# A fused attention and mixture-of-experts kernel: turns of y one iteration later, logits in four column quarters

## Chip, cores and metric

The kernel runs on one core of a Trainium2 chip. The metric is the device time of one execution in microseconds (us). TensorE (PE, with its weight loads as PEld), VectorE (DVE), ScalarE (ACT) and GpSimd (POOL) each work through their own instructions in order; SyncE (SP) issues most of the DMAs.

## What is computed

Linear attention with a gated state, then a layer of eight experts of which each token takes two, then a dense layer with h - tanh(h). Cut to what matters:

```python
f = 1 / (1 + exp(-f_logit))                      # q, k, v, f_logit: (4, 8, 768, 48)
for t in range(768):
    state = f[t][:, None] * state + outer(k[t], v[t])     # per batch and head
    y[t] = q[t] @ state
x = y as 3072 tokens of 384
logits = x @ w_gate                              # 8 experts
noisy = logits + log1p(exp(x @ w_noise)) * noise
top 2 of noisy, their softmax as weights
out = sum of weight * (relu(x @ w1[e]) @ w2[e]) over the two experts
h = out @ w_in;  result = (h - tanh(h)) @ w_out
```

## The kernel before

The stages are the attention (to about 162 us), the experts with two blocks of tokens each, and the dense layer. The change lies in the attention. Its 24 chunks j = 4c + b are 128 time steps of one batch b with all eight heads; heads are packed in pairs, four pairs a = 0..3 of 128 partitions (2 x 64, 48 of each 64 used).

The loop over j (L540) issues a software pipeline in the order of the code; no scheduler moves anything, since `manual_schedule` is on, so each engine's order is the order of these calls:

- `scores(j + 1)`: products of keys and queries into two PSUM banks pA (b3, b4), then DVE multiplies by the triangular mask (am).
- `scaled(j + 2)`: ACT makes exp of the accumulated decay and its inverse (epos, eneg); DVE scales the keys (kqT L325), POOL the queries (kqT L327).
- `post(n)`: POOL scatters rows of finished chunks to their experts' places in DRAM (L513), two in most iterations, more near the end.
- `decay(j + 3)`: ACT exp and ln, DVE scan (fc).
- `x_split(j - 1)`: ACT copies the turned y to f16 (xkeep L408), DVE the remainder (xkeep L409).
- when chunk j - 1 ends a group of four: `group_logits`, the product of the gate weights with y of the whole group, into bank b7, which ACT copies (lgT).
- `outputs(j)`: state times queries (L367) and am times values (L371, the two heads of a pair in the two column halves of the array) into bank b5; ACT copies to yT (L376).
- `group_rows`: the logits are turned to rows of tokens on PE and copied by ACT (lgs); `route` is a generator that picks the two experts and the places, and `advance(n)` issues a few of its steps at several places of an iteration. Its first DVE step is nl (L452), behind two ACT steps (ex).
- `key_rows(j + 1)`, `states(j)`: turned keys, their products with the values (pK, bank b6), DVE sum (tsum), POOL scaling of the state (L395). They don't exist for the last four chunks.
- `x_rows(j)`: PE turns y of chunk j into the single bank b0 (pX). It needs the copy yT of chunk j and the split of chunk j - 1, which empties b0.

Behind the loop come the split of the last chunk and the first expert products; `load_x(0, 0)`, issued by SP in iteration 21, brings the first block of expert 0 from DRAM when the scatters so far have landed, `load_x(0, 1)` the second when all have. An fp32 product is two passes of the array, so it shows as two records.

Of the kernel before, what the change touches and what calls it, by code (L numbers as in the profile page):

```python
# [8 lines left out]
F32 = mybir.dt.float32  # L9
# [5 lines left out]
AF = mybir.ActivationFunctionType  # L15
# [5 lines left out]
B, H, S, D = 4, 8, 768, 48  # L21
N, DM, NE, FF, F2 = 3072, 384, 8, 1024, 2048
NCH = S // 128
NT = B * NCH
CAP = 832
GN = 4 * 16 + NT * NE
# [45 lines left out]
def fast(ctx, tc, flag, f_cols, kq_cols, v_rows, gates, blank, w12, w_in, w_out, out):  # L72
# [179 lines left out]
    with ExitStack() as actx:  # L252
# [35 lines left out]
        wgn = gn[:, 0:64].rearrange("p (a c) -> p a c", a=4)  # L288
        nz = gn[:, 64:].rearrange("p (c b e) -> p c b e", c=NCH, b=B)
# [124 lines left out]
        def logits(g):  # L414
            y = T["yT", g]
            p = ps.tile([128, 96], F32, name="pt", tag="b7")
            for a in range(4):
                nc.tensor.matmul(p, y[:, a, 0, :], gn[:, 16 * a:16 * a + 96], start=(a == 0), stop=(a == 3))
            nc.scalar.activation(lgs[:, groups[g][0], :], p[:, :16], AF.Copy)

        def group_logits(g):
            G = len(groups[g])
            p = ps.tile([16, 4, 128], F32, name="pt", tag="b7")
            for a in range(4):
                nc.tensor.matmul(p[:, :G], wgn[:, a, :], T["yT", g][:, a, :G, :], start=(a == 0), stop=(a == 3))  # L425
            t = T["lgT", g] = work.tile([16, 4, 128], F32, name="lgT", bufs=1)
            nc.scalar.activation(t[:, :G], p[:, :G], AF.Copy)

        def group_rows(g):
            G = len(groups[g])  # L430
            j0 = groups[g][0]
            t = T.pop(("lgT", g))
            p = ps.tile([128, 4, 16], F32, name="pt", tag="b7")
            for i in range(G):
                nc.tensor.transpose(p[:, i, :], t[:, i, :], ident[:16, :16])
            nc.scalar.activation(lgs[:, j0:j0 + G, :], p[:, :G], AF.Copy)
# [103 lines left out]
        for j in range(NT):  # L540
# [6 lines left out]
            scores(j + 1)  # L547
            scaled(j + 2)
# [21 lines left out]
            x_rows(j)  # L570
# [3 lines left out]
            if 4 <= j < 20 and not j % 2:  # L574
                split_weights(0, (j - 4) // 2)
        x_split(NT - 1)
# [536 lines left out]
def packed_rows(q, k, v, f_logit, w_gate, w_noise, noise, w1, w2):  # L1113
# [12 lines left out]
    wgn = np.zeros((2, 64, 4, 16), w_gate.dtype)  # L1126
    for w, at in ((w_gate, 0), (w_noise, NE)):
        wgn[:, :D, :, at:at + NE] = w.reshape(4, 2, D, NE).transpose(1, 2, 0, 3)
    gates[:, 0:64] = wgn.reshape(128, 64)
    gates[:, 64:] = noise.reshape(B, NCH, 128, NE).transpose(2, 1, 0, 3).reshape(128, NT * NE)  # L1130
# [30 lines left out]
```

## Time and profile before

| what | us |
|---|---|
| median of 3 runs (960.32 to 962.53) | 960.33 |
| profiled execution | 962.88 |
| its span | 960.8 |
| PE busy | 937.8 (98%) |
| ACT busy | 606.1 (63%) |
| DVE busy | 595.6 (62%) |
| POOL busy | 155.9 (16%) |

The busy times are of the whole span; the attention has other shares than the rest, so they are read by stretch. A busy PE counts the tails of its pipelined products too.

### The profile page before, as it was taken

What the parts mean: (1) busy time and instruction counts of PE and PEld (TensorE: products, weight loads), DVE (VectorE), ACT (ScalarE), POOL (GpSimd) and SP (SyncE); (2) the same over time, 40 slices, a digit from 0 to 9 for tenths busy, and PEclk for the clock granted to TensorE, in tenths of its full rate; (3) what the DMA queues carried; (4) which work ended last, traced back from release to release, by engine and by line L of the source; (5) the groups of instructions that cost most, each with busy time, mean ns of one, the idle gap of its engine ahead of it and who ended that gap; (6) DMA issues with size and microseconds to landing.
All of it is one profiled execution on the core that took longest, in us unless ns stands there. A gap on an engine that the chain in (4) does not pass through costs nothing.

```text
span 960.8 us, 16249 instructions
## 1 busy us (share of the span) xinstructions
PE 937.8 (98%) x5950; PEld 552.8 (58%) x5950; DVE 595.6 (62%) x1260; ACT 606.1 (63%) x1558; POOL 155.9 (16%) x198
## 2 busy tenths in 40 slices
PE   8999998999999999999999999999999999999997
PEld 7677776555656555555656654555555555555553
DVE  7677884366555555566676666556565565664664
ACT  6666673285656656585858567666666666666663
POOL 3357776300000000000000035200301101000000
PEclk9999999999999999999999999999999999999999
DMA  7757754656465645555564275302212121110001
GB/s 279 263 201 246 263 195 159 174 175 196 132 181 132 189 143 153 155 158 155 147 167 110 82 194 144 71 25 58 75 42 49 43 59 42 42 26 1 33 1 37
DMA packets 111801, 120.04 MB, mean 125 GB/s; under 512 B 66400, under 2 KB 89568, under 8 KB 111584
## 3 DMA queue, kind: packets, MB, share of 16 engines
q1 hardware_dynamic: 105280, 99.64, 35.9%
q0 software_dynamic: 6144, 18.88, 6.2%
q8 instruction: 48, 0.79, 0.3%
q10 hardware_dynamic: 288, 0.39, 0.1%
q14 instruction: 41, 0.34, 0.1%
HBM read 76.41 MB, written 29.88 MB: 111 GB/s over the span
## 4 chain that ended last, share of the span: by engine, by line
PE 88%; DVE 7%; ACT 2%; issue 2%; DVEq 0%
PE py L202 41%; PE ph L187 40%; PE pt L425 2%; DVE fc L314 2%; PE pA L341 2%; DVE am L343 1%; PE pX L402 1%; DVE kqT L325 1%; PE pK L526 1%; PE pY L367 1%; DVE xkeep L409 1%; PE pY L371 1%; ACT yT L376 0%; DVE tsum L390 0%; DVE pr L491 0%
## 5 line engine op out<-in xcount | busy, mean ns | idle before, releaser
L202 PE MATMUL py<-wsplit,hs 128*128 128x384 f16 x2432 | 432.3, 326 | 0.6 <-DVE hs L688 0.6
L202 PEld LDWEIGHTS <-hs 128*128 128x128 f16 x2432 | 238.1, 98 | 172.2 <-issue 1.4
L187 PE MATMUL ph<-xt,wsplit 128*128 128x512 f16 (+3 forms) x1152 | 224.2, 340 | 0.0
L187 PE MATMUL ph<-xt,winS 128*128 128x512 f16 x864 | 201.6, 379 | 0.0
L187 PEld LDWEIGHTS <-wsplit 128*128 128x128 f16 x1152 | 112.7, 98 | 86.4 <-issue 0.5
L220 DVE SCALAR_TENSOR_TENSOR hs<-ph,hs 128x256 f16<-128x256 f32 (+2 forms) x192 | 79.7, 443 | 120.5 <-ACT hs L212 120.2
L679 DVE SCALAR_TENSOR_TENSOR s<-s,z 128x512 f32<-128x512 f32 x96 | 66.5, 692 | 141.6 <-ACT s L676 141.6
L212 ACT ACTIVATE hs<-ph 128x512 f16<-128x512 f32 (+3 forms) x128 | 65.8, 514 | 134.4 <-PE ph L187 131.7
L646 POOL DMA_INDIRECT g<-y_rows,yslot x48 | 48.3, 1006 | 580.6 <-DMA y_rows<-yo 394.3
L675 ACT ACTIVATE z<-ph 128x512 f32<-128x512 f32 x96 | 57.2, 596 | 130.0 <-PE ph L187 130.0
L187 PEld LDWEIGHTS <-winS 128*128 128x128 f16 x864 | 84.4, 98 | 91.9
L147 DVE SCALAR_TENSOR_TENSOR wsplit<-raw,wsplit 128x768 f16<-128x768 f32 x72 | 70.9, 985 | 13.9 <-ACT wsplit L146 12.6
L151 ACT ACTIVATE junk<-wsplit 128x384 f16<-128x384 f16 x144 | 74.4, 516 | 2.3
L676 ACT ACTIVATE s<-z,bias_a 128x512 f32<-128x512 f32 x96 | 69.3, 722 | 3.1
L681 DVE SCALAR_TENSOR_TENSOR g<-s,ph 128x512 f32<-128x512 f32 x96 | 65.9, 687 | 3.3
L688 DVE TENSOR_TENSOR hs<-g,hs 128x512 f16<-128x512 f32 x96 | 65.7, 684 | 0.1
L146 ACT ACTIVATE wsplit<-raw 128x768 f16<-128x768 f32 x72 | 59.9, 832 | 0.5 <-DMA raw<-wo_f 0.5
L687 ACT ACTIVATE hs<-g 128x512 f16<-128x512 f32 x96 | 58.8, 613 | 1.1 <-DVE g L681 1.1
L513 POOL DMA_INDIRECT xs<-xkeep,yslot x48 | 51.6, 1074 | 15.5 <-issue 9.1
L343 DVE TENSOR_TENSOR am<-pA,tri 128x512 f32<-128x512 f32 x48 | 30.8, 684 | 12.3 <-PE pA L341 12.1
L327 POOL TENSOR_TENSOR kqT<-eneg,kq 128x512 f32<-128x512 f32 x23 | 31.8, 1384 | 12.0 <-ACT eneg L323 11.6
L376 ACT ACTIVATE yT<-pY 128x512 f32<-128x512 f32 x24 | 14.3, 596 | 27.1 <-PE pY L371 25.6
(147 smaller groups left out, 877.0 us busy)
## 6 DMA issues: line engine op xcount, KB each, us to landing
raw<-in_w SPq DMA_DIRECT2D x64, 384.0 KB, 3.6
kq<-in_kq_cols SPq DMA_DIRECT2D x24, 512.0 KB, 5.8
y_rows<-yo SPq DMA_DIRECT2D x47, 192.0 KB, 1.9
f<-in_f_cols SPq DMA_DIRECT2D x24, 256.0 KB, 3.9
w<-in_moe_w_out SPq DMA_DIRECT2D x32, 192.0 KB, 3.3
w<-in_moe_w_in SPq DMA_DIRECT2D x24, 256.0 KB, 3.4
v<-in_v_rows SPq DMA_DIRECT2D x24, 192.0 KB, 2.7
out<-o SPq DMA_DIRECT2D x22, 192.0 KB, 2.0
```

The source lines that it names most:

```text
L146: nc.scalar.activation(t[:, 0], raw, AF.Copy, scale=SW)
L147: nc.vector.scalar_tensor_tensor(t[:, 1], raw, SW, t[:, 0], op0=OP.mult, op1=OP.subtract)
L151: nc.scalar.activation(junk[:, :DM], RING[e, f][:, 0, 3 * i:3 * i + 3, :].rearrange("p a b -> p (a b)"), AF.Square, accum_out=wsum[:, 8 * ...
L187: nc.tensor.matmul(ph[:, :n], l, x[:, r, :n], start=(o == 0), stop=(o == 8))
L202: nc.tensor.matmul(p[:max(m, 128)], l, r, start=(f == 0 and o == 0), stop=(f == last and o == len(ops) - 1))
L212: nc.scalar.activation(hs[:, :n], ph[:, :n], AF.Relu, accum_out=hacc[:, at:at + 1])
L220: nc.vector.scalar_tensor_tensor(hs[:, at:at + hi - lo], ph[:, lo:hi], 0.0, hs[:, lo:hi], op0=OP.max, op1=OP.subtract)
L676: nc.scalar.activation(s, z, AF.Square, scale=1.0 / SZ, bias=bias_a)
L679: nc.vector.scalar_tensor_tensor(s, s, ZD, z, op0=OP.add, op1=OP.mult)
L681: nc.vector.scalar_tensor_tensor(g, s, 0.5, ph, op0=OP.mult, op1=OP.mult)
L687: nc.scalar.activation(hs[:, :512], g, AF.Copy)
L688: nc.vector.tensor_tensor(hs[:, 512:], g, hs[:, :512], op=OP.subtract)
```

## The change

The turn of y of chunk j leaves its place at the end of iteration j and stands in iteration j + 1 behind the scores; the last turn stands behind the loop. The gate weights are padded from 16 to 32 columns. The logits of a group are no longer 4 products of 16 rows by 512 columns but 16 of 32 rows by 128 columns: chunk i of the group goes to partitions 32i to 32i + 31 of the PSUM tile, one column quarter of the array. The logits then lie on 128 partitions and are turned in one piece. The logits of the last chunk take the 32 padded columns.

```diff
-        wgn = gn[:, 0:64].rearrange("p (a c) -> p a c", a=4)
-        nz = gn[:, 64:].rearrange("p (c b e) -> p c b e", c=NCH, b=B)
+        wgn = gn[:, 0:128].rearrange("p (a c) -> p a c", a=4)
+        nz = gn[:, 128:].rearrange("p (c b e) -> p c b e", c=NCH, b=B)
...
         def logits(g):
             y = T["yT", g]
-            p = ps.tile([128, 96], F32, name="pt", tag="b7")
+            p = ps.tile([128, 32], F32, name="pt", tag="b7")
             for a in range(4):
-                nc.tensor.matmul(p, y[:, a, 0, :], gn[:, 16 * a:16 * a + 96], start=(a == 0), stop=(a == 3))
+                nc.tensor.matmul(p, y[:, a, 0, :], wgn[:, a, :], start=(a == 0), stop=(a == 3))
...
         def group_logits(g):
             G = len(groups[g])
-            p = ps.tile([16, 4, 128], F32, name="pt", tag="b7")
+            p = ps.tile([128, 128], F32, name="pt", tag="b7")
             for a in range(4):
-                nc.tensor.matmul(p[:, :G], wgn[:, a, :], T["yT", g][:, a, :G, :], start=(a == 0), stop=(a == 3))
-            t = T["lgT", g] = work.tile([16, 4, 128], F32, name="lgT", bufs=1)
-            nc.scalar.activation(t[:, :G], p[:, :G], AF.Copy)
+                for i in range(G):
+                    nc.tensor.matmul(p[32 * i:32 * i + 32], wgn[:, a, :], T["yT", g][:, a, i, :], start=(a == 0),
+                                     stop=(a == 3))
+            t = T["lgT", g] = work.tile([128, 128], F32, name="lgT", bufs=1)
+            nc.scalar.activation(t[:32 * G], p[:32 * G], AF.Copy)
 
         def group_rows(g):
...
-            p = ps.tile([128, 4, 16], F32, name="pt", tag="b7")
-            for i in range(G):
-                nc.tensor.transpose(p[:, i, :], t[:, i, :], ident[:16, :16])
-            nc.scalar.activation(lgs[:, j0:j0 + G, :], p[:, :G], AF.Copy)
+            p = ps.tile([128, 4, 32], F32, name="pt", tag="b7")
+            nc.tensor.transpose(p[:, :G].rearrange("p g c -> p (g c)"), t[:32 * G], ident[:32 * G, :32 * G])
+            nc.scalar.activation(lgs[:, j0:j0 + G, :], p[:, :G, :16], AF.Copy)
...
             scores(j + 1)
+            if j:
+                x_rows(j - 1)
             scaled(j + 2)
...
             states(j)
-            x_rows(j)
             advance(rate)
...
+        x_rows(NT - 1)
         x_split(NT - 1)
```

The order on PE in iteration 4, the first with a group's logits, before. The names are those of the list above: pX is the turn, pA the scores of the next chunk (eight products, the last two stand here), L425 the logits, L435 their turning.

```order
L341 MATMUL pA_622<-kqT 128x128
L341 MATMUL pA_623<-kqT 128x128
L425 MATMUL pt<-yT,gn 16x512 x4
L367 MATMUL pY<-kqT,st_160 128x128 x4
L371 MATMUL pY<-am,v 48x128 x8
L435 MATMUL pt<-ident,lgT 128x16 x4
L354 MATMUL pkr<-ident,kqT 128x128 x4
L386 MATMUL pK<-v,krows 128x96 x4
L402 MATMUL pX<-ident,yT 128x128 x4
L341 MATMUL pA_722<-kqT 128x128
```

The same place now:

```order
L341 MATMUL pA_617<-kqT 128x128
L341 MATMUL pA_618<-kqT 128x128
L402 MATMUL pX<-ident,yT 128x128 x4
L426 MATMUL pt<-yT,gn 32x128 x16
L367 MATMUL pY<-kqT,st_160 128x128 x4
L371 MATMUL pY<-am,v 48x128 x8
L436 MATMUL pt<-ident,lgT 128x128
L354 MATMUL pkr<-ident,kqT 128x128 x4
L386 MATMUL pK<-v,krows 128x96 x4
L341 MATMUL pA_726<-kqT 128x128
```

The turn of chunk 4 no longer stands between the states (pK) and the next scores; in front of the logits there is the turn of chunk 3 instead. The logits are 16 short products for 4 long ones, and one turn replaces four.

The second place is the end of the loop on PE, iterations 22 and 23, from the scores of chunk 23 to the first expert product (L187), before:

```order
L341 MATMUL pA_2124<-kqT 128x128
L367 MATMUL pY<-kqT,st_162 128x128 x4
L371 MATMUL pY<-am,v 48x128 x8
L402 MATMUL pX<-ident,yT 128x128 x4
L425 MATMUL pt<-yT,gn 16x384 x4
L367 MATMUL pY<-kqT,st_163 128x128 x4
L371 MATMUL pY<-am,v 48x128 x8
L435 MATMUL pt<-ident,lgT 128x16 x3
L187 LDWEIGHTS wsplit
```

and now:

```order
L341 MATMUL pA_2164<-kqT 128x128
L402 MATMUL pX<-ident,yT 128x128 x4
L367 MATMUL pY<-kqT,st_162 128x128 x4
L371 MATMUL pY<-am,v 48x128 x8
L402 MATMUL pX<-ident,yT 128x128 x4
L426 MATMUL pt<-yT,gn 32x128 x12
L367 MATMUL pY<-kqT,st_163 128x128 x4
L371 MATMUL pY<-am,v 48x128 x8
L436 MATMUL pt<-ident,lgT 128x96
L187 LDWEIGHTS wsplit
```

Here the turn of chunk 21 has come in behind the scores; that of chunk 22 stands where it stood, since there are no more scores, key rows or states in between. The order on ACT, DVE and POOL is the same before and after.

## Rows read from the trace of the kernel before

**Rows 1.** Stretches: us, length, busy (instructions) of each engine, clock, DMA share, GB/s.

```profile
180.00:500.00 320.00, 320.00 (x1879) 183.70 (x1878) 191.05 (x430) 207.78 (x617) 0.00 (x0) 1.00 0.58 163
60.92:87.26 26.34, 25.00 (x243) 19.32 (x242) 21.16 (x49) 18.02 (x40) 19.08 (x26) 1.00 0.72 241
```

**Rows 2.** PE in that group (start, us, what, [idle before]); a wait; a line's records.

```profile
60.92 1.16 PE L341 MATMUL pA<-kqT 64*128 64x128 f32 x16
62.01 3.61 PE L425 MATMUL pt<-yT,gn 128*16 128x512 f32 x8
65.55 1.16 PE L367 MATMUL pY<-kqT,st 128*128 128x128 f32 x8
66.64 1.08 PE L371 MATMUL pY<-am,v 128*48 128x128 f32 x16
67.65 0.42 PE L435 MATMUL pt<-ident,lgT 16*128 16x16 f32 x4
68.00 0.66 PE L354 MATMUL pkr<-ident,kqT 128*128 128x128 f32 x4
68.49 1.03 PE L386 MATMUL pK<-v,krows 128*128 128x96 f32 x8
69.36 0.60 PE L402 MATMUL pX<-ident,yT 128*128 128x128 f32 x4
69.89 1.16 PE L341 MATMUL pA<-kqT 64*128 64x128 f32 x16
...
PE pX L402 <- DVE xkeep L409: 8.0, 12, 0.9
...
L371 PE MATMUL pY<-am,v x384: 272/273/311, 15.1 to 161.8; 128*48 128x128 f32 x192
```

**Rows 3.** DVE in the same group, timeline.

```profile
62.11 1.29 DVE L343 TENSOR_TENSOR am<-pA,tri 128x512 f32<-128x512 f32 x2 [1.26 <-PE pA L341]
...
65.12 0.53 DVE L409 SCALAR_TENSOR_TENSOR xkeep<-pX,xkeep 128x384 f16<-128x384 f32 x1
69.03 0.19 DVE L452 TENSOR_TENSOR nl<-ex,gn 128x32 f32<-128x32 f32 x1 [3.38 <-ACT ex L450]
...
82.95 1.29 DVE L343 TENSOR_TENSOR am<-pA,tri 128x512 f32<-128x512 f32 x2 [0.29 <-PE pA L341]
```

**Rows 4.** A stretch of the start, iterations 1 to 3, columns as in rows 1.

```profile
18.32:34.64 16.32, 13.52 (x149) 11.01 (x148) 12.61 (x23) 12.76 (x27) 6.37 (x7) 1.00 0.91 292
```

**Rows 5.** DVE and POOL timeline before the end of the loop.

```profile
133.93 0.56 DVE L390 TENSOR_TENSOR tsum<-pK,st 128x384 f32<-128x384 f32 x1
...
134.57 1.47 POOL L395 TENSOR_TENSOR st<-tsum,gall 128x384 f32<-128x384 f32 x1 [0.50 <-DVE tsum L390]
...
150.22 1.28 POOL L327 TENSOR_TENSOR kqT<-eneg,kq 128x512 f32<-128x512 f32 x1
```

**Rows 6.** PE timeline at the end of the loop; a stretch behind it, as rows 1.

```profile
152.71 1.16 PE L341 MATMUL pA<-kqT 64*128 64x128 f32 x16
...
157.25 2.75 PE L425 MATMUL pt<-yT,gn 128*16 128x384 f32 x8
...
162.32 1.64 PE L187 MATMUL ph<-xt,wsplit 128*128 128x384 f16 x9
...
169.61 0.18 PE L475 MATMUL pt<-sel,before 128*128 128x8 bf16 x1 [2.01 <-DVE sel L461]
...
169.67 2.40 PE L187 MATMUL ph<-xt,wsplit 128*128 128x384 f16 x9
...
170.30:173.70 3.40, 3.40 (x13) 1.61 (x11) 1.55 (x6) 1.08 (x4) 2.78 (x5) 0.51 0.42 160
```

**Rows 7.** Loads of xt from 178.0 to 183.5 us: issues, landing; PE, first use.

```profile
L176 SPq DMA_TRANSPOSE xt<-xs x2: 1217/1392/1566, 179.5 to 180.7; - x2
...
DMA to landing us min/median/max: 3.4/4.0/4.5
...
188.90 1.87 PE L187 MATMUL ph<-xt,wsplit 128*128 128x448 f16 x9
```

More of the change, by code (lines that the diff above doesn't have):

```diff
@@ L25 @@
 CAP = 832
-GN = 4 * 16 + NT * NE
+GN = 4 * 32 + NT * NE
 EARLY = 16
@@ L1125, in packed_rows @@
     gates = np.zeros((128, GN), w_gate.dtype)
-    wgn = np.zeros((2, 64, 4, 16), w_gate.dtype)
+    wgn = np.zeros((2, 64, 4, 32), w_gate.dtype)
     for w, at in ((w_gate, 0), (w_noise, NE)):
         wgn[:, :D, :, at:at + NE] = w.reshape(4, 2, D, NE).transpose(1, 2, 0, 3)
-    gates[:, 0:64] = wgn.reshape(128, 64)
-    gates[:, 64:] = noise.reshape(B, NCH, 128, NE).transpose(2, 1, 0, 3).reshape(128, NT * NE)
+    gates[:, 0:128] = wgn.reshape(128, 128)
+    gates[:, 128:] = noise.reshape(B, NCH, 128, NE).transpose(2, 1, 0, 3).reshape(128, NT * NE)
     w12 = np.empty((NE * 8, 128, 2 * DM), w1.dtype)
```

## The prediction

> **What bounds the kernel now.** I read the stretches first. From 180 us on TensorE has no idle time at all, 320.00 us busy of 320.00 [rows 1], and nothing of the change lies there. So the change can only move the end of the attention stage, and what it takes off that end it takes off the program.
>
> Inside the stage the unit is four iterations, one group of chunks: 26.34 us, PE busy 25.00, DVE 21.16, ACT 18.02, POOL 19.08 [rows 1]. The PE timeline of the group that starts at 60.92 gives the price of each step as the distance from its start to the next start [rows 2]: scores 1.09, logits 3.54, outputs 1.09 and 1.01, turning the logits back 0.35, key rows 0.49, states 0.87, turn of y 0.53. Without the logits and their turning an iteration is 5.08 us of PE, four are 20.3. With 3.54, 0.35 and 0.13 for the route's small products the group needs 24.3; the other 2.0 are idle. Nearly all of it stands before the turns of y: 8.0 us in twelve waits for the DVE half of the split (xkeep) [rows 2], because the turn needs the one PSUM bank that the split of the chunk before has to empty.
>
> The DVE timeline of the same group closes the loop [rows 3]. DVE multiplies the scores by the mask (am), scales the keys, scans, splits; the split ends at 65.65, 3.54 us after am began. Then the turn may go, behind it stand the next scores, and behind those the next am: PE and DVE take turns. DVE's idle time in the group is 1.26 and 0.29 before am, and 3.38 before nl, the first DVE step of the routing, which stands for the chain logits, copy, turn, copy, exp, ln. That is 4.93; so DVE needs 26.34 - 4.93 = 21.4 us per group without a wait.
>
> **The turns of y, moved.** Nothing is added or removed: 24 turns, the same DVE, ACT and POOL order; on PE each turn now stands behind the next chunk's scores. The scores no longer wait for the split, so the loop is open. Where does the stall go? The turn of chunk j-1 now starts 1.09 us after scores j+1 start and ends 0.53 later, at +1.6; the ACT half of its split could start at +1.2 before, so ACT may wait 0.5 us there. Cover: ACT's next step but the logit copy is the copy of the outputs, which waits for PE until about +3.8; without that cover the price would be 0.5 an iteration. DVE reaches its half at +4.2 (65.12 against 60.92), so it is not delayed. No DMA and no POOL instruction is passed. Next late is DVE itself.
>
> **The logits in quarters.** Before: 4 products of 512 columns, each two passes, 3.54 us [rows 2]. Now: 16 products of 128 columns, 32 passes, four at a time if the quarters work side by side. The nearest row is the output product (L371), whose two column halves run side by side: 16 passes of 128 columns, 8 rounds, 1.01 us including the change of tile. Eight rounds of four are the same length, so X = 1.02. Bounds: two at a time, 16 rounds, 2.04; one after another as now, 3.54. Nothing in the trace is cheaper than 8 rounds of such passes, and I see no gain below it. I take 1.02, the row in which column tiles are seen at work. The Trainium skill ("TensorE: Matmul & The Clock Gate", Measured speedup vs the span model) gives 3.07 times for four row tiles; by that an estimate of X is 3.54 / 3.07 = 1.15, and the sum would end 0.5 us later. No run here shows four tiles. One turn instead of four of the logits: 0.35 becomes about 0.15 (a full turn is 0.53 / 4). The wider gate table is one small load at the start. The last chunk's logits with 32 columns instead of 96 save at most 0.2 off a chain that waits elsewhere, counted at nothing.
>
> **A group afterwards.** PE needs 20.3 + 1.02 + 0.15 + 0.13 = 21.7 (with the 0.56 that some turns take). DVE needs 21.4 plus its wait for nl. Counted from the start of the scores, nl may go at 1.09 + 0.53 + 1.02 + 1.09 + 1.01 + 1.38 = 6.1 (the last term is 67.65 to 69.03, copies and exp, unchanged); DVE gets there at 65.65 - 60.92 = 4.7. The wait is 1.4 instead of 3.4. If PE runs ahead of DVE it shrinks, but not far: the turn still needs the split of the chunk before. From the end of that split nl takes 0.06 + 0.53 + 1.02 + 2.10 + 1.38 = 5.1, DVE 0.5 (state sum [rows 5]) + 3.54 = 4.0, so 1.1 stays. DVE per group: 22.5 to 22.8. That is more than PE's 21.7, so DVE is the bound; POOL (19.1) and ACT (18.0) are below. I take 22.5, a gain of 3.84 per group.
>
> **The sum.** Start: the three iterations from 18.32 to 34.64 last 16.32 with PE busy 13.52 [rows 4]; DVE and ACT are below that. The idle 2.8 go, and the iteration before them loses its turn, 0.6: 3.4. The DMA share there is 0.91, so the loads have little room, but they are issued one to two iterations ahead; if they bound, 1 of the 3.4 is lost. Groups: from 34.64 to the state sum of chunk 18 at 133.93 are 99.3 us, 3.77 groups, x 3.84 = 14.4. Tail: from that state sum on, POOL has an unbroken string, 134.57 to the end of the last scaled queries at 151.50 [rows 5]: 16.9 us of state updates, queries and eight scatters that the change doesn't touch. With 0.7 of hand-over scores 23 can't start sooner than 17.6 behind the state sum; now it is 18.8 (152.71). Gain 1.1; PE, which needs some 13.5 for its part, will stand idle there for about 4 us. From scores 23 to the first expert product are 9.61 us [rows 6]; one turn comes in (0.53), the logits of three chunks fall from 2.7 to 0.8, their turning by 0.2: gain 1.5.
>
> The clock: after an idle 2.01 us, with little work before it, the granted clock stands at 0.51, the 1.2 GHz level, for 3.4 us [rows 6], and nine expert products take 2.40 instead of 1.64: half of 3.4, 1.7 us, lost. The idle 4 us before scores 23 are longer, so I count one such fall as new: -1.7. The old one stays.
>
> 3.4 + 14.4 + 1.1 + 1.5 - 1.7 = 18.7 us.
>
> Is it kept? The second token block of expert 0 lands at 180.7 + 4.5 = 185.2 and is used at 188.90 [rows 7]: 3.7 us of room. It hangs on POOL's string, which moves by 3.4 + 14.4 = 17.8; PE moves by 18.7 and uses 0.9 of the room. After that everything is paced by PE. The profiled execution lasted 962.88 us, its span 960.8; the median of the runs is 960.33, its lower end, and I take the gain off that: 960.33 - 18.7 = 941.6.
>
> **Rivals.**
> PE bound: DVE's wait for nl vanishes or the clock doesn't fall. For: PE's 21.7 and DVE's 22.5 are close. Against: the bank of the turn ties PE to the split. Groups of 21.7 give 3.0 more, no fall 1.7 more: 936.9.
> Two quarters at a time: the trace shows two tiles, never four. X = 2.04, and each us of X goes into nl's wait: 3.77 x 1.02 = 3.8, and 0.7 in the tail: 946.1. The same time comes from DVE and POOL stretching each other more when they stand denser.
> The quarters do not run side by side, so half of the change does nothing: X = 3.54, 3.77 x 2.52 = 9.5, tail 1.9: 953.0. The turns alone then bring 7. Against it: the output product [rows 2].
> Slower: the array empties before each change of quarter, so every pass stands alone with its full length of 273 ns [rows 2]: X = 32 x 0.273 = 8.7, 7.7 more for each of the 3.77 groups and the tail: 36 us lost, 978. It decides from X = 5 on, where 4.8 x (X - 1.02) eats the 18.7. Against it: between the column halves of L371 no such price is paid, 16 passes in 1.01 us. The Trainium skill ("TensorEngine Tiling (Array Packing)", Key Properties) says that a change of tiling mode drains the array, but a change of tile in one mode doesn't; by that only the way into and out of the logits pays, as L371 does, and the trace agrees with its 1.01.
>
> **How the numbers follow.** Forecast 0.58; PE bound 0.12; two at a time or more contention 0.17; no overlap 0.09; the array empties 0.02; between the last two, near no change, 0.02. The range takes the first three with their bounds, 936.5 to 947.5, and leaves 0.13 out. About 0.3%, 2.9 us, is what a measurement can tell from no change: faster by more 0.96, within 0.02, slower 0.02.
>
> **What would show it.** PE's waits for xkeep before the turns gone, scores following states without a gap; L426 at about 1.0 us per group; groups of 22.5 with DVE idle 1.1 to 1.4 before nl and hardly anywhere else; iterations of 4.5 at the start; scores 23 waiting some 4 us for POOL's queries; xt ready before its use. Wrong would be: logits near 2 or 3.5 us, PE waiting for xkeep as long as now, ACT's split copy delaying the copy of the outputs, or idle PE before the second block.

## The result

The changed kernel takes 949.98 us (median of four, 948.68 to 951.29), the kernel before 960.36 beside it (960.32 to 962.53, four runs): ratio 0.9886 [0.9867, 0.9906]. Faster, as forecast, but by 10.4 us and not by 18.7; the time lies 2.5 us above the range. On two other chips, run again beside the experiments, the ratio is 0.9859 [0.9840, 0.9878] and 0.9862 [0.9846, 0.9879], a gain of 13.2 and 12.7.

The profiled execution lasted 948.68 (before 962.88). From the first expert product to the end both need the same: 162.32 to 960.8 before, 148.28 to 946.5 now, 798.5 and 798.2. So 14.0 of the 14.3 us between the two traces lie in the attention.

PE in the iteration with a group's logits after the change, the answer to [rows 2] (start, us, what):

```profile
30.59 1.16 PE L341 MATMUL pA<-kqT 64*128 64x128 f32 x16
31.69 0.66 PE L402 MATMUL pX<-ident,yT 128*128 128x128 f32 x4
32.27 1.08 PE L426 MATMUL pt<-yT,gn 128*32 128x128 f32 x32
33.28 1.16 PE L367 MATMUL pY<-kqT,st 128*128 128x128 f32 x8
...
35.38 0.33 PE L436 MATMUL pt<-ident,lgT 128*128 128x128 f32 x1
35.55 0.60 PE L354 MATMUL pkr<-ident,kqT 128*128 128x128 f32 x4
...
36.95 0.82 PE L341 MATMUL pA<-kqT 64*128 64x128 f32 x9
```

The logits, 32 passes in four quarters, take 33.28 - 32.27 = 1.01 us; the turning of the logits 0.17. PE's waits for the split before the turns are nearly gone: 8.0 us in twelve over the whole attention before [rows 2], now (8 to 175 us) 1.4 in three:

```profile
PE pX L402 <- DVE xkeep L409: 1.4, 3, 0.5
```

The scores of chunk 5 start at 30.59, 4.05 earlier than before. Then come four groups, from these scores to those of chunks 9, 13, 17 and 21, columns as in [rows 1] (DVE is the third busy time, POOL the fifth, the granted clock the third number from the right):

```profile
30.59:52.85 22.26, 21.75 (x263) 19.21 (x262) 20.65 (x50) 17.78 (x38) 9.93 (x10) 1.00 0.83 285
52.85:78.15 25.30, 23.42 (x264) 20.72 (x263) 25.13 (x51) 17.83 (x39) 20.96 (x25) 0.93 0.76 252
78.15:100.42 22.27, 21.75 (x264) 19.21 (x263) 20.82 (x49) 17.61 (x38) 19.11 (x25) 1.00 0.86 275
100.42:124.10 23.68, 21.47 (x260) 18.84 (x259) 23.51 (x50) 17.21 (x37) 19.45 (x24) 1.00 0.76 258
```

Two groups are as long as forecast (22.5), the second and the fourth are not. The first has few POOL instructions, 10 for 24 or more later, since the scatters start only at its end (52.55). In the second DVE is busy for 25.13 us of 25.30, with 51 instructions where the others have 49 or 50. Its clock is 0.93, not 1.00: PE stands 1.32 us for a step of DVE that comes late behind a long one (both below), and then the state products run at the lower level, 0.50 of the clock from 68 to 70 us:

```profile
68.17 1.91 PE L367 MATMUL pY<-kqT,st 128*128 128x128 f32 x8
```

The forecast had no fall of the clock inside the groups. In after_third, a repeat with the same long DVE steps in this group and a clock of 1.00, it lasts 24.2, so up to 1.1 us of the 25.3 may be the clock's. The DVE groups of lines between 30 and 150 us say which instructions last longer. Now (busy, mean ns):

```profile
L147 DVE SCALAR_TENSOR_TENSOR wsplit<-raw,wsplit 128x768 f16<-128x768 f32 x8 | 12.9, 1618 | 0.0
...
L328 DVE TENSOR_TENSOR gall<-eneg,own 128x8 f32<-128x8 f32 x18 | 6.9, 386 | 0.0
```

Before, over the same stretch:

```profile
L147 DVE SCALAR_TENSOR_TENSOR wsplit<-raw,wsplit 128x768 f16<-128x768 f32 x8 | 9.7, 1208 | 0.0
...
L328 DVE TENSOR_TENSOR gall<-eneg,own 128x8 f32<-128x8 f32 x18 | 3.0, 167 | 0.0
```

The first is the remainder of expert 0's weight split (`split_weights`, every second iteration, at its end), the second the copy of the decay at the chunk's end (gall, in `scaled`, 8 elements wide); I call them weight split and gate copy. Both read two operands from SBUF, as POOL's state update and queries do. Together they are 7.1 us longer. The other DVE lines of the stretch are at most 0.01 us longer in mean. A gate copy that lasts 1.75 us and the POOL steps beside it:

```profile
55.76 0.84 POOL L395 TENSOR_TENSOR st<-tsum,gall 128x384 f32<-128x384 f32 x1
56.11 1.75 DVE L328 TENSOR_TENSOR gall<-eneg,own 128x8 f32<-128x8 f32 x1
56.55 1.28 POOL L327 TENSOR_TENSOR kqT<-eneg,kq 128x512 f32<-128x512 f32 x1
```

The timeline around the longest weight split of the changed kernel (DVE and POOL):

```profile
60.09 0.54 DVE L390 TENSOR_TENSOR tsum<-pK,st 128x384 f32<-128x384 f32 x1
60.12 0.97 POOL L514 DMA_INDIRECT xs<-xkeep,yslot  x1 [0.21 <-issue]
...
60.89 3.11 DVE L147 SCALAR_TENSOR_TENSOR wsplit<-raw,wsplit 128x768 f16<-128x768 f32 x1
61.11 0.84 POOL L395 TENSOR_TENSOR st<-tsum,gall 128x384 f32<-128x384 f32 x1
61.90 1.27 POOL L327 TENSOR_TENSOR kqT<-eneg,kq 128x512 f32<-128x512 f32 x1
...
63.92 1.28 DVE L343 TENSOR_TENSOR am<-pA,tri 128x512 f32<-128x512 f32 x2
```

And the same place before:

```profile
69.77 0.54 DVE L390 TENSOR_TENSOR tsum<-pK,st 128x384 f32<-128x384 f32 x1
...
70.39 0.83 POOL L395 TENSOR_TENSOR st<-tsum,gall 128x384 f32<-128x384 f32 x1 [4.41 <-DVE tsum L390]
...
70.57 1.47 DVE L147 SCALAR_TENSOR_TENSOR wsplit<-raw,wsplit 128x768 f16<-128x768 f32 x1
71.33 1.85 POOL L327 TENSOR_TENSOR kqT<-eneg,kq 128x512 f32<-128x512 f32 x1
```

Before, POOL is idle when the state sum (tsum) comes; its state update (st) starts at once, ahead of the weight split, which ends 0.8 us after the update's end; the queries behind it last 1.85 instead of 1.27. The three take turns. Now a scatter still runs when the sum is there. The update begins 0.22 us after the weight split's recorded start, the queries follow back to back, and the split ends 0.83 us after the queries' end: it has stood still for both.

The end of the loop (answer to [rows 6]):

```profile
138.52 1.16 PE L341 MATMUL pA<-kqT 64*128 64x128 f32 x16 [3.72 <-POOL spacer L513]
139.61 1.11 PE L402 MATMUL pX<-ident,yT 128*128 128x128 f32 x4
140.52 1.92 PE L367 MATMUL pY<-kqT,st 128*128 128x128 f32 x8
142.36 1.39 PE L371 MATMUL pY<-am,v 128*48 128x128 f32 x16
```

PE stands 3.72 us for POOL's string, then the turns last 1.11 instead of 0.66 and the state products 1.92 instead of 1.06 (as at 60.41 and 60.90 in the same trace). The granted clock of that stretch stands third from the right (columns of [rows 1]):

```profile
139.60:143.70 4.10, 4.10 (x30) 3.65 (x28) 2.09 (x5) 0.49 (x1) 0.00 (x0) 0.58 0.88 182
```

It is 0.58: mostly the lower level, 1.2 GHz, after an idle 3.72 us.

### The profile page after: what moved, and what is told of

Read it like the earlier page. It is cut to its first block, busy times and chain, and to the rows that moved or that the text cites. A ratio compares the mean times of both kernels' runs of the same rounds, so it can differ in the third digit from the quotient of the medians.

```text
span 946.5 us, 16487 instructions
## 1 busy us (share of the span) xinstructions
PE 922.9 (98%) x6069; PEld 555.2 (59%) x6069; DVE 602.5 (64%) x1260; ACT 604.3 (64%) x1558; POOL 158.3 (17%) x198
## 4 chain that ended last, share of the span: by engine, by line
PE 87%; DVE 5%; POOL 3%; issue 2%; ACT 1%; DMA 1%; SPq 0%; POOLq 0%; DVEq 0%
PE py L202 42%; PE ph L187 40%; POOL xs L514 2%; PE pY L371 1%; DVE am L343 1%; PE pA L341 1%; POOL kqT L327 1%; PE pY L367 1%; DVE fc L314 1%; PE pX L402 1%; PE pK L386 1%; DMA kq<-in_kq_cols 1%; POOL st L395 1%; DVE kqT L325 1%; DVE xkeep L409 0%
## 5 line engine op out<-in xcount | busy, mean ns | idle before, releaser
L187 PE MATMUL ph<-xt,wsplit 128*128 128x512 f16 (+3 forms) x1152 | 223.9, 339 | 0.0
L187 PE MATMUL ph<-xt,winS 128*128 128x512 f16 x864 | 201.7, 379 | 0.0
L187 PEld LDWEIGHTS <-wsplit 128*128 128x128 f16 x1152 | 112.8, 98 | 86.2 <-issue 0.2
L187 PEld LDWEIGHTS <-winS 128*128 128x128 f16 x864 | 84.4, 98 | 91.9
L147 DVE SCALAR_TENSOR_TENSOR wsplit<-raw,wsplit 128x768 f16<-128x768 f32 x72 | 74.2, 1031 | 13.8 <-ACT wsplit L146 12.4
L514 POOL DMA_INDIRECT xs<-xkeep,yslot x48 | 55.2, 1150 | 15.2 <-issue 9.2
L341 PE MATMUL pA<-kqT 64*128 64x128 f32 x384 | 27.9, 284 | 8.9 <-POOL spacer L513 4.9
```

Of the source, the lines that this page charges most:

```text
L147: nc.vector.scalar_tensor_tensor(t[:, 1], raw, SW, t[:, 0], op0=OP.mult, op1=OP.subtract)
L187: nc.tensor.matmul(ph[:, :n], l, x[:, r, :n], start=(o == 0), stop=(o == 8))
L514: sc = nc.gpsimd.indirect_dma_start(out=xs, out_offset=bass.IndirectOffsetOnAxis(ap=yslot[:, r, j:j + 1], axis=0), in_=T["x16", j], in_off ...
```

## Experiments

The stage is read by two marks of each trace, which do not depend on the chip as far as seen (the kernel before has its first expert product at 162.32 and 162.28 on two chips): the four groups between the scores of chunks 5 and 21, and the start of the first expert product. On chips B and C the kernels need 804 to 810 us behind that mark instead of 797 to 801, and the kernel before takes 973 to 974 there in all, so times stand as ratios to the kernel before on the same chip. The kernel before was not traced on those two.

| kernel | chip, before | time | ratio [95%] | groups | first expert product |
|---|---|---|---|---|---|
| before | A 960.36 | | 1 | 26.3, 26.3, 26.3, 26.3 | 162.3 |
| changed | A 960.36 | 949.98 | 0.9886 [0.9867, 0.9906] | 22.3, 25.3, 22.3, 23.7 | 148.3 |
| turns_only | B 974.07 | 963.48 | 0.9908 [0.9878, 0.9938] | 24.8, 24.9, 24.9, 24.5 | 154.1 |
| quarters_only | B | 967.67 | 0.9934 [0.9905, 0.9962] | 23.8, 24.8, 23.9, 23.9 | 151.8 |
| splits_late | B | 954.48 | 0.9808 [0.9784, 0.9832] | 21.7, 22.9, 23.0, 22.6 | 145.9 |
| posts_first | B | 977.25 | 1.0042 [1.0024, 1.0060] | 26.1, 29.6, 29.6, 29.4 | 165.7 |
| after_again | C 973.00 | 959.81 | 0.9859 [0.9840, 0.9878] | 22.3, 24.8, 23.9, 23.7 | 149.5 |
| splits_ahead | C | 961.90 | 0.9889 [0.9871, 0.9907] | 22.2, 25.9, 24.2, 24.3 | 151.0 |
| queries_early | C | 958.69 | 0.9862 [0.9823, 0.9901] | 23.4, 25.4, 24.1, 23.7 | 149.8 |
| splits_late_queries_early | C | 954.42 | 0.9824 [0.9803, 0.9845] | 22.3, 22.2, 23.0, 22.7 | 147.7 |
| before_again | D 961.20 | 962.41 | one run | 26.3, 26.3, 26.3, 26.3 | 162.3 |
| posts_batched | D | 970.64 | one run | 22.3, 30.5, 30.5, 30.2 | 168.3 |
| gall_pool | D | 952.27 | 0.9904 [0.9887, 0.9921] | 22.1, 26.8, 23.7, 24.8 | 152.7 |
| gall_pool_splits_late | D | 945.63 | 0.9841 [0.9827, 0.9856] | 21.7, 21.7, 22.2, 22.7 | 143.7 |
| before_six | E 962.61 | 975.22 | one run | 27.4, 30.4, 30.5, 30.6 | 176.6 |
| posts_moved | E | 946.29 | 0.9832 [0.9815, 0.9849] | 22.3, 22.6, 22.5, 22.2 | 145.7 |
| splits_late_again | E | 946.32 | 0.9833 [0.9819, 0.9846] | 22.3, 23.0, 22.9, 22.5 | 146.2 |
| posts_moved_splits_late | E | 949.22 | 0.9863 [0.9846, 0.9880] | 22.3, 22.9, 23.6, 23.2 | 148.1 |
| after_third | F 962.71 | 949.98 | 0.9862 [0.9846, 0.9879] | 22.3, 24.2, 24.1, 23.7 | 149.5 |
| posts_moved_queries_early | F | 947.89 | 0.9848 [0.9832, 0.9865] | 22.3, 22.6, 22.5, 22.2 | 142.8 |

### The two halves of the change, each alone

turns_only is the kernel before with the moved `x_rows`, quarters_only the kernel before with the new logits.

```diff
 turns_only, on the kernel before
+            if j:
+                x_rows(j - 1)          # behind scores(j + 1)
-            x_rows(j)                  # behind states(j)
...
+        x_rows(NT - 1)                 # behind the loop
 quarters_only: the diff of the change without these lines
```

> The turns of y moved as in the change, the logits as before (4 products of 512 columns). Theory A (port): DVE operations whose operands all lie in SBUF (the remainder of a weight split, gall) stand still while POOL runs the state update and the scaled queries, and the change makes these two run back to back in some groups. The prediction's rival of no overlap, 953, then comes out late by the same stretching: 952 to 957, some splits of 3.1 us. Theory B (the losses come from POOL's string of scatters or from falls of the clock, the stretched DVE operations are a by-product): 952 to 954, PE's waits mostly for POOL.

> The logits in quarters, the turns of y where they were. The logits fall from 3.54 to 1.01 us in five groups and 2.7 to 1.0 in the sixth, all in front of DVE's wait for nl: up to 2.5 x 4 in the loop and some in the tail, 949 to 952. Theory A: PE and DVE still take turns through the bank of the turn, so POOL's queries wait for ACT as before, and the weight splits stay at 1.47 and 0.95. Theory B has no reason for another length either, but expects the tail's wait for POOL's string to come up here too, 952 to 955.

The times expected were for chip A. By ratio the turns bring 0.9%, the quarters 0.7%, and both together 1.1 to 1.4%. The five runs of quarters_only spread from 962.6 to 968.9, and its ratio is the poorer for it: as a time on chip A it is 954, outside the 949 to 952 of theory A and inside the 952 to 955 of theory B. The first expert product, which is not touched by what follows it, says more: the turns bring it forward by 8.2 us, the quarters by 10.5, together the 18.7 of the forecast, but the changed kernel has it only 12.8 to 14.0 earlier. The two halves lose something only where they stand together. The waits between 30 and 130 us show what each half leaves. With the turns alone, DVE still waits for the chain of the long logits, 2.7 us a group:

```profile
DVE nl L452 <- ACT ex L450: 10.8, 4, 3.8
```

With the quarters alone, the turns still stand between split and scores:

```profile
PE pX L402 <- DVE xkeep L409: 8.0, 11, 1.7
```

Each half works as its step of the prediction says. In both kernels every weight split is 1.47 or 0.95 long, as before; the splits of 3.1 expected of turns_only did not come. Of these three kernels only the changed one has them. The gate copies are another matter: turns_only has three of 1.58 to 1.74 in the loop.

### Taking the weight split out of the loop, or out of the collision

splits_late does expert 0's splits in iterations 20 to 23; posts_first gives POOL the scatters before the queries; splits_ahead puts the split ahead of the state sum.

```diff
 splits_late
-            if 3 <= j < 19 and j % 2: load_weights(0, (j - 3) // 2)
-            if 4 <= j < 20 and not j % 2: split_weights(0, (j - 4) // 2)
+            if j >= 20: split_weights(0, 2 * j - 40); split_weights(0, 2 * j - 39)
+            (load_weights(0, ...) in iterations 17 to 22)
 posts_first
-            scaled(j + 2)
             post(...)
+            scaled(j + 2)
 splits_ahead
+            if 4 <= j < 20 and not j % 2: split_weights(0, (j - 4) // 2)   # ahead of states(j)
             states(j)
```

> The changed kernel with the eight weight splits of expert 0 (one ACT copy, one DVE remainder each) and their loads moved from iterations 4 to 18 to iterations 20 to 23, two in each. Theory A: no 3.1 us split is left in the loop, every group of four iterations takes 21.7 to 22.5 us instead of 22.3 and 25.3 or 23.7 in turn; scores of chunk 21 near 119 instead of 124, time 944 to 947. Theory B: the groups stay as unequal as they are, scores of chunk 21 at 122 to 124, time 948 to 951.

> The changed kernel with the scatters of an iteration issued ahead of the scaled queries, so that POOL has state update, two scatters, queries instead of state update, queries, two scatters. Theory A: the state update and the queries no longer follow each other at once, DVE gets in between, no split longer than 1.5 and no gall longer than 0.9; the queries come 2.6 us later and scores may wait for them; 944 to 950. Theory B: POOL's string is as long as it was, the scores wait longer for the queries, 950 to 956.

> The changed kernel once more, beside its variants on one chip. Theory A (DVE's weight split and gate copies are stretched where POOL's state update and queries run back to back with them): the same two long weight splits of 3.1 us, the same two slow groups of four, first expert product at 148 to 151, ratio to before 0.987 to 0.991. Rival B (the slow groups of the first profile were chance of that execution, and the forecast of 18.7 us was right): groups of 22.3 everywhere, first expert product at 144, ratio 0.981.

> The weight split of expert 0 stands one step earlier on DVE and ACT, ahead of the state sum, where POOL has no tensor operation released yet; nothing else is changed. A: no weight split of 3.1 us is left in the iterations from 4 to 19, each 1.5 or less; the two slow groups fall by 1 to 3 us, first expert product 2 to 4 us earlier than in the repeated changed kernel, ratio to it 0.996 to 0.998. Rival (a long weight split comes from its own input or from ACT's half and not from POOL): the 3.1 stay wherever the split stands, time within 0.1%. Second rival: the state sum, now behind the split, comes 1.5 late in every second iteration and POOL's queries with it: 0 to 4 us slower.

splits_late: groups of 21.7 to 23.0 and the best ratio on its chip. It takes the whole splits out of the loop, though, two in each group, and not only what they grew by, so it cannot tell how much the stretch alone costs. posts_first missed the times of both theories: no weight split over 1.47, but the queries are late, PE waits 15.2 us for them, and eight gate copies of 1.5 to 1.77 come in their place, each beside the end of a scatter and the queries alone. after_again agrees with the theory on chip C: the slow groups are not chance, and a third weight split is 3.1 long.

splits_ahead answers whether the long split is the split's own affair. The same instruction, four places earlier, beside a running scatter:

```profile
59.70 0.97 POOL L514 DMA_INDIRECT xs<-xkeep,yslot  x1 [0.21 <-issue]
59.92 0.96 DVE L147 SCALAR_TENSOR_TENSOR wsplit<-raw,wsplit 128x768 f16<-128x768 f32 x1 [0.17 <-ACT wsplit L146]
```

All eight are 0.95 or 0.96 long. So neither its input nor ACT's half nor a scatter stretches it. The time does not fall, though, and the groups stay at 22.2 to 25.9: the state sum now stands behind the split, and scores wait 3.7 us for gate copies and 1.9 for keys, all on DVE (the second rival had them wait for POOL's queries). So this run does not show that a long split costs time; that rests on posts_moved below.

### Which step of POOL, and when

posts_batched puts the scatters of a group into one iteration of four; gall_pool moves the gate copy to POOL; gall_pool_splits_late has no weight split in the loop as well.

```diff
 posts_batched
-            post({18: 3, 19: 3, 20: 8, 23: 4}.get(j, 2))
+            post({23: 4}.get(j, 8 if j % 4 == 1 else 0))
 gall_pool
-            nc.vector.tensor_tensor(gall[:, j], ...)
+            nc.gpsimd.tensor_tensor(gall[:, j], ...)
```

> The kernel before, for its stage on the chip of the variants. Stage as in the first profile: scores of chunk 5 at 34.6, groups of 26.3, weight splits 1.47 and 0.95 in turn, gate copies 0.16 to 0.2, first expert product at 162 to 164. If the chip itself is slower in the attention stage, all of these are later; if the 13 us by which its times are longer lie behind the stage, they show between the first expert product and the end.

> The scatters of a group stand as eight in a row in one iteration of four instead of two in each; the same number in all. It shows what stretches DVE's weight split. Theory A (POOL's state update and queries, back to back, hold DVE off): in iterations without scatters POOL takes the state update as soon as the state sum is there and the queries right behind it, just when the weight split starts, so six to eight of the eight weight splits last 2.5 to 3.1 us. Rival (the scatters' descriptor work on POOL stretches it): in iterations without scatters the split is 0.95 to 1.0 long. The eight in a row hold up the queries: the group is 2 to 6 us longer than in the changed kernel by either theory.

> The gate copy of each chunk (gall, 128 x 8) is made by POOL behind the queries instead of by DVE; nothing else is changed. A (in the slow groups DVE loses some 1.5 us at a gate copy that waits out POOL's work, and the scores behind it wait as well): the slow groups fall from 25 to 23.5, PE has no wait over 1 us for DVE before scores but the one behind a weight split, the first expert product 2 to 4 us earlier than in the repeated changed kernel (149.5), ratio to before 0.982 to 0.985. Rival (POOL's string sets the pace, with its hand-overs between instructions some 21 to 22 us per group): POOL gains six to eight tenths per iteration and the groups stay or grow; ratio 0.986 to 0.990.

> The gate copies on POOL and expert 0's weight splits in iterations 20 to 23: both DVE steps that were seen to stretch are out of the loop. A: no DVE operation between 30 and 120 us is stretched; groups of 21.5 to 22.5, as forecast for the change without the stretch (22.5), the scores of chunk 21 at 117 to 120 (121.05 with the late splits alone), ratio to before 0.977 to 0.981. Rival (POOL's string is the bound): groups of 22.5 to 23.5 and the same time as with the late splits alone, 0.980 to 0.983.

posts_batched refuted the theory as I had it: no weight split is over 1.47, in iterations where POOL has nothing but update and queries. The lines say why:

```profile
59.77 0.83 POOL L395 TENSOR_TENSOR st<-tsum,gall 128x384 f32<-128x384 f32 x1 [3.94 <-DVE tsum L390]
...
59.95 1.46 DVE L147 SCALAR_TENSOR_TENSOR wsplit<-raw,wsplit 128x768 f16<-128x768 f32 x1
60.71 1.85 POOL L327 TENSOR_TENSOR kqT<-eneg,kq 128x512 f32<-128x512 f32 x1
```

POOL waits, the update starts before the split, and the split gets in between: the order of the kernel before. So it is not the nearness of the two POOL operations that costs, but that POOL comes late. (The group is 30 us long because eight scatters in a row hold up the queries: PE waits 20.1 us for them in three waits.)

gall_pool missed its time (0.9904 for 0.982 to 0.985; the rival had 0.986 to 0.990): without the gate copy on DVE, weight splits of 3.0 to 3.5 us remain, POOL's string is longer by one step, and the first expert product comes at 152.7. With the splits gone too, the groups are 21.7, 21.7, 22.2 and 22.7. In the second PE is busy throughout, in the third all but 0.4 us:

```profile
51.59:73.25 21.66, 21.66 (x263) 19.20 (x262) 20.02 (x42) 16.04 (x36) 20.24 (x27) 1.00 0.76 247
73.25:95.44 22.19, 21.78 (x263) 19.21 (x263) 22.02 (x44) 16.32 (x36) 20.62 (x29) 1.00 0.82 247
```

My sentence that nothing on DVE would be stretched was wrong: the scan, 1.21 us in the other kernels, now meets POOL's pair.

```profile
76.30 0.84 POOL L395 TENSOR_TENSOR st<-tsum,gall 128x384 f32<-128x384 f32 x1
76.41 3.04 DVE L314 TENSOR_TENSOR_SCAN fc<-carry,fc 128x512 f32<-128x512 f32 x1
77.08 1.28 POOL L327 TENSOR_TENSOR kqT<-eneg,kq 128x512 f32<-128x512 f32 x1
```

So the step with two SBUF operands that DVE has reached at that moment stands still, here for 1.8 us, although POOL's update began first; POOL had come from a scatter here too. The third and the fourth group, each with such a scan, are 0.5 and 1.0 us longer than the second. From the first expert product on this kernel needs 801.0 us instead of 798, and 945.63 is 15.6 below before, not the 18.6 of its first expert product: the ratio misses the 0.977 to 0.981 expected, and where the 3 us go stays open.

### POOL's slack, taken away and given back

before_six is the kernel before, with six scatters in iterations 8, 12 and 16 and 1, 0, 1 in the three behind each; posts_moved is the changed kernel with 0, 2, 3, 3.

```diff
 before_six, on the kernel before
-            post({18: 3, 19: 3, 20: 8, 23: 4}.get(j, 2))
+            post({18: 3, 19: 3, 20: 8, 23: 4}.get(j, 2 if j < 8 or j > 19 else (6, 1, 0, 1)[j % 4]))
 posts_moved, on the changed kernel
+            post({18: 3, 19: 3, 20: 8, 23: 4}.get(j, 2 if j < 8 else (0, 2, 3, 3)[j % 4]))
```

> The kernel before, with six scatters instead of two in every fourth iteration (8, 12, 16, those with the routing's logits) and 1, 0, 1 in the others; the order on PE is the old one. Theory A (a weight split is stretched where a scatter still runs on POOL when the state sum is there, because the state update and the queries then follow back to back): the weight splits of these iterations, near 70, 97 and 124 us, last 3.1 instead of 1.47, though nothing of the change is in; POOL does not wait for the state sum in front of them. Rival (the long splits belong to the new order on PE and DVE): they stay at 1.47.

> The changed kernel, with no scatter in the iterations 8, 12 and 16 and 2, 3, 3 in the three behind each; the same number in all. A: POOL is idle when the state sum of these iterations comes, the state update starts ahead of the weight split, the queries behind it: all weight splits 1.5 or less; the slow groups fall by about 1.6, first expert product 1.5 to 4 us earlier than in the changed kernel (148.3 to 149.5), ratio to before 0.982 to 0.987. Rival: the collision only moves to another DVE step with two operands in SBUF (gate copy or scan), and the groups stay within 0.5.

> The late weight splits once more, beside the next kernel on one chip. Groups of 21.7 to 23.0 and the first expert product at 145.9 as in its first profile; ratio 0.981 to 0.985 whichever chip it is.

> Late weight splits and moved scatters. If the collisions that are left with late splits (gate copies of 0.85 to 1.2, one in each group) come from POOL being late in the iterations with the logits, they go, groups are 21.7 to 22.3, and the first expert product is 0.5 to 2 us earlier than with late splits alone. Rival: with three scatters in a row POOL's queries are late elsewhere and PE waits there for POOL: 0 to 3 us slower than late splits alone.

before_six, with PE's old order and long logits, has the long splits, 3.42 us each at 71, 102 and 132 us:

```profile
70.39 0.54 DVE L390 TENSOR_TENSOR tsum<-pK,st 128x384 f32<-128x384 f32 x1
...
70.72 0.97 POOL L513 DMA_INDIRECT xs<-xkeep,yslot  x1 [0.22 <-issue]
...
71.19 3.42 DVE L147 SCALAR_TENSOR_TENSOR wsplit<-raw,wsplit 128x768 f16<-128x768 f32 x1
71.72 0.84 POOL L395 TENSOR_TENSOR st<-tsum,gall 128x384 f32<-128x384 f32 x1
```

posts_moved, with the change in, has none:

```profile
60.59 0.83 POOL L395 TENSOR_TENSOR st<-tsum,gall 128x384 f32<-128x384 f32 x1 [2.88 <-DVE tsum L390]
...
60.77 1.47 DVE L147 SCALAR_TENSOR_TENSOR wsplit<-raw,wsplit 128x768 f16<-128x768 f32 x1
```

So the change is neither needed for the stretch nor enough for it: what decides is whether POOL is still scattering when the state sum is there. All traces with the splits in their place in the loop say the same, 112 splits in fourteen executions: 17 last 3.0 to 3.5, and each time a scatter runs past the end of the state sum; 39 last 1.46 or 1.47, and each time POOL is idle and waits for the sum. The other 56 are issued right behind the state sum and last 0.95 to 0.97. DMA traffic does not tell them apart: the queues are busy 0.84 to 0.98 during the long splits of the changed kernel and of before_six, 0.84 to 1.03 during seven of 1.47 in the changed kernel, in posts_moved and in the kernel before. In posts_moved the groups are 22.2 to 22.6, the 22.5 of the forecast, and the state sum of chunk 18 stands at 116.52, 17.4 earlier than before; the forecast was 17.8. The moved scatters alone bring the ratio from 0.9886, 0.9859 or 0.9862 on chips A, C and F to 0.9832 on chip E, where the changed kernel itself did not run; the intervals of C and F reach into that of E. The first expert product, 145.7 for 148.3 to 149.5, moves the same way, by 2.6 to 3.8 us. The late splits reach the same 0.9833. Both together don't add (0.9863, 2.9 us slower than the late splits alone): with three scatters in a row gate copies of 2.47 appear. That is the time of the rival, but PE waits there for gate copies and not for POOL's queries.

### The tail

queries_early and its two companions put the scatters of iteration 20 behind the last scaled queries.

```diff
 queries_early
-            post({18: 3, 19: 3, 20: 8, 23: 4}.get(j, 2))
+            post({18: 3, 19: 3, 20: 0, 21: 8, 23: 4}.get(j, 2))
```

> The scatters of iteration 20 are issued one iteration later, behind the last scaled queries (chunk 23) on POOL; nothing else is changed. Theory on the tail (POOL's string holds up scores 23, PE is idle 3.7 us before it and the clock falls behind that): scores 23 comes 3 to 5 us earlier, the idle time before it is under 1 us, and no products at half clock stand behind it; the first expert product is 4 to 6 us earlier, 142 to 144, if its rows land in time; time 3 to 5 us below the repeated changed kernel. Rival: the scatters end 1.3 us later than now and the first block of rows lands later than the weights and logits need it, so that PE waits for it: 0 to 2 us.

> Both edits that were seen to bear on the stage: expert 0's weight splits in iterations 20 to 23, and the scatters of iteration 20 behind the last scaled queries. If DVE's stretched splits and POOL's string are the two causes of the missing gain, they add: groups of 22 to 23, scores 23 without a wait over 1 us, first expert product at 141 to 143, ratio to before 0.976 to 0.979. Rival: the first block of rows is what the expert part then waits for, and only 0 to 2 us are won over the late splits alone: 0.979 to 0.981.

> The changed kernel a third time, to stand beside the next one. Ratio to before 0.985 to 0.990; two or three slow groups, first expert product at 148 to 150.

> Moved scatters, and those of iteration 20 behind the last scaled queries. If TensorE's wait before the last scores and the clock fall behind it are what the tail costs: scores 23 come 3 to 5 us earlier than 135.9, no products at half clock behind them, first expert product at 141 to 143 (145.7 with moved scatters alone), ratio 0.979 to 0.982. Rival: the last scatters end later and the first block of rows lands later, so that the expert products, or a later step that needs those rows, wait: ratio 0.982 to 0.985.

The first two ran on chip C. The scores of chunk 23 do come early (3.8 and 5.0 us behind those of chunk 22 instead of 7.6), but ACT stands still for up to 5.1 and 6.7 us at the passage to the experts. It does so there in after_again too, with no releaser on this core that the profile knows:

```profile
156.27 0.60 ACT L376 ACTIVATE yT<-pY 128x512 f32<-128x512 f32 x1 [6.95 <-remote]
```

Both missed the first expert product that was expected (149.8 and 147.7), and they decide nothing on the tail. On chip F they do. With moved scatters and early queries:

```profile
130.52 1.16 PE L341 MATMUL pA<-kqT 64*128 64x128 f32 x16
...
142.81 2.98 PE L187 MATMUL ph<-xt,wsplit 128*128 128x384 f16 x9 [3.94 <-DMA xt<-xs]
```

The scores come 5.4 us earlier than in posts_moved (135.89), without a wait and without half speed behind them. Then PE waits 3.94 us for the rows of the first block, which the scatters behind the queries delay, and the clock falls there instead: the rival. Of 5.4 us, 2.9 reach the first expert product and none that can be measured reaches the end (0.9848 beside 0.9832 on another chip).

## Why the prediction missed

**What bound the kernel: right.** The wait of the turn for the split, and of nl for the logits, were the two idle times of the loop; quarters_only keeps the one and turns_only the other.

**The logits: right.** X = 1.01 us (forecast 1.02), the turning 0.17 (0.15). Four quarters work side by side; the rivals of 2.04, 3.54 and 8.7 us fall.

**The start: right,** 4.05 instead of 3.4.

**The group of 22.5: the step that failed.** "DVE needs 26.34 - 4.93 = 21.4 us per group without a wait" was summed from a trace in which POOL waits for DVE, and taken as a constant. And "POOL (19.1) and ACT (18.0) are below" compared POOL's busy time with the group. The waits of POOL in the group from 60.92 to 87.26 before the change read:

```profile
POOL st L395 <- DVE tsum L390: 5.6, 4, 4.4
POOL xs L513 <- issue: 1.7, 9, 0.2
```

With the hand-overs between its instructions POOL occupies 19.1 + 1.7 = 20.8 of 26.34 us; 5.6 are slack, 4.4 of them at the one state sum behind the logits. The change takes 2.6 us off exactly the iteration that held this slack (from 8.97, 60.92 to 69.89 [rows 2], to 6.36) and 1.5 off the other three together. Then POOL comes late there, keeps DVE out for its two operations in a row, and DVE, the bound, gets longer: 23.51 and 25.13 us busy instead of 20.7. From the scores of chunk 5 to the state sum of chunk 18 the gain is 99.29 - (120.61 - 30.59) = 9.3 us instead of 14.4. These 5.1 us, less the 0.65 that the start brought beyond its forecast, are the miss within the traces, 14.0 instead of 18.7. A part of them, up to 1.1 in the second group, may be PE at the lower clock behind its wait for DVE; the runs do not part the two.

The rival named it, DVE and POOL "stretching each other more when they stand denser", with a price of 4.5 us; the traces show 4.7. That the price fits is luck: it had been worked out for two quarters at a time, and no row of the stretch stood behind it. What was missing was a reason to give it more than the smaller part of 0.17: the profile of before had one, since its weight splits were 1.47 and 0.95 in turn, and the queries beside the longer ones 1.85 instead of 1.27.

The Trainium skill ("SBUF — State Buffer", Who interferes with whom) says that a DVE instruction with two SBUF inputs and a GpSimd instruction that reads SBUF contend for a port that is an exclusive lock; its section "SBUF: two separate sides" says that the one that starts first has it for its whole length. The first agrees with the rows: 1.47 is the 0.65 that the update still has to run, then 0.82 of the split. The second agrees where POOL was idle before. In the splits of 0.95 DVE starts first and the update behind it lasts 1.47 instead of 0.84 (134.57 in [rows 5]):

```profile
134.40 0.95 DVE L147 SCALAR_TENSOR_TENSOR wsplit<-raw,wsplit 128x768 f16<-128x768 f32 x1
```

Where POOL comes from a scatter it does not agree: the split is recorded as started 0.22 us before the update and still waits for update and queries, 3.11 us. Why is not shown.

**The tail: right.** The scores of chunk 23 start 17.9 us behind the state sum of chunk 18 (120.61 to 138.52; forecast 17.6), the idle time before them is 3.7, and 1.2 before those of chunk 22 (forecast about 4), and turns and outputs at the lower clock last 1.11 + 1.92 + 1.39 = 4.4 instead of 2.8: 1.6 lost, forecast 1.7. From scores 23 to the first expert product 9.76 us, forecast 9.61 - 1.5 + 1.7 = 9.8.

**Is it kept: right.** Behind the first expert product nothing is lost, 798.5 and 798.2.

**The base: right as a number.** The median beside the result is 960.36, the forecast took 960.33. But the terms were worked out from an execution of 962.88, 2.5 above it, and the two traces differ by 14.2 (962.88 to 948.68) where the medians differ by 10.4; another 1.3 lies between the profiled execution of after and its median. So of the 8.35 us between 941.63 and 949.98, 4.5 are the traces' and 3.8 the choice of executions. The medians of before on chips D to F are 961.20, 962.61 and 962.71, so 960.36 may have been low. The repeats show a third long split and 1.2 us more up to the first expert product, which is of the size of the 1.3, but it was not seen in the runs of the median itself.

## What to carry to other kernels

The busy sum of the engine that is to become the bound is only a floor for the phase in which it was measured: operations that read two SBUF operands on DVE, beside such operations on POOL, changed length here with the order in which POOL and DVE came to them. Before a wait is removed, list who else was waiting in that same iteration; an engine that looks free by its busy time may be living on that wait. Here, moving POOL's scatters out of that one iteration was worth 0.3 to 0.5% (0.9859 to 0.9886 on three chips against 0.9832 on a fourth) beside the 1.1 to 1.4% of the change itself, for one line.

## Hardware seen on the way

A DVE operation held off by two POOL operations in a row grows by about the length of both: weight splits of 0.95 alone, 1.47 behind one, 3.0 to 3.5 behind two, a gate copy of 0.16 up to 2.47, a scan of 1.21 up to 3.19 (in gall_pool). A scatter by itself does not hold a weight split off (0.96 beside one in splits_ahead). But where the state update stands ready behind the scatter, the split makes no headway during the rest of the scatter either: with 0.07, 0.22, 0.53 and 0.61 us from its start to the update's, the splits last 3.00, 3.11, 3.42 and 3.50, each time 2.9 from the update's start on. On chips B and C the kernel before takes about 12 us longer, the kernels traced there need 5 to 11 us more behind the first expert product, and what the traces show of it is ACT standing idle at the passage to the experts without a releaser on this core (6.95 us at once); the cause stays open.
